# Attention plus gated MLP on one core: split value-weight loads, V and K products by column half, and fixed PSUM banks for the attention products

## The chip, the cores and the metric

The kernel runs on one core of a Trainium2 chip. The metric is the device time of one execution in microseconds (us), as the median of several runs. Single profiled executions give a trace; their span is 1.5 to 2 us shorter than the time, because the time also covers starting and ending the program.

PE is TensorE, ACT ScalarE, DVE VectorE, POOL GpSimd, SP the engine that issues all loads and stores on its one queue.

## The reference

A layer norm of x (2048 tokens, 640 features) feeds two branches, a linear attention with softmax feature maps (32 heads of 20) and a gated MLP (inner width 1536). Both are added to x. Cut to what matters:

```python
xn  = layernorm(x)
qkv = xn @ wqkv                      # q, k, v: 32 heads of 20
phi = lambda u: concat(softmax(u @ w_phi), softmax(-(u @ w_phi)))
kv  = phi(k)^T v ;  z = sum of phi(k) over the tokens       # per head
o   = phi(q) kv / (phi(q) z + 1e-6)
out = x + o @ wo + (silu(xn @ w1) * (xn @ w3)) @ w2
```

## The kernel before

The kernel does not multiply q and k by `w_phi`. It folds `w_phi` into the weights: the **first fold** makes `Wkp` for K, the **second fold** makes `Wqp` for Q. Each fold needs its part of wqkv transposed (`wqkT`), which a transposing load brings. Tiles of 128 tokens are numbered 0 to 15. K8 is the K product of tile 8, V8 its V product, ten matmuls of 320 columns each. An **MLP chunk** is one call of `mlp`: ten matmuls of 512 columns.

The parts that the change and the argument touch (cuts marked with `# ...`):

```python
class _Program:
    # ... records every operation with what it reads and writes, finds the dependencies
    def ready(self, ops):            # when PE could start these ops without waiting inside them
        t, off = 0.0, 0.0
        for o in ops:
            if o.eng != "PE":
                continue
            for d in self.find_deps(o):
                t = max(t, d.end + 0.07 - off)
            off += o.cost
        return t
    def commit(self, ops):
        # ...
            if o.dma:
                # ... one model of the queue: a rate, and a fixed time to land
                self.bus = max(self.bus, t + 0.5) + o.cost / (280e3 if o.part else 320e3)
                o.end = self.bus + 1.6

def first_loads():
    load_x(0, 1)
    load_x(1, 2)
    load_x(2, 4)
    P.dma("SP", wv[:], wqkv_t[:, :, 2 * D:3 * D])
    w13(0, 512)                                  # first third of w1 and w3: chunks 0 to 3
    P.dma("SP", phi_s[:], phi_t)
    P.dma("SP", wqkT[:, DC:2 * DC, :], A_wqkv[:, D:2 * D], True)     # for the first fold
    load_x(4, 8)
    load_x(8, 12)

def proj(t, w, k):                               # V and K products of one token tile
    for i in range(DC):                          # DC = 5 row chunks of the weights
        for q in range(2):                       # 2 column halves, one PSUM bank each
            mm(bank(k + q, 320), xnT[:, i, t * 128:(t + 1) * 128],
               w[:, i, 320 * q:320 * q + 320], i == 0, i == DC - 1)

def banks(n):                                    # the n neighbouring banks that come free first
    # ...

def loads():
    # ... for t in 4 to 15: transpose x tile t into xnT by DMA; and among them:
        if t == 7:
            yield lambda: (w13(512, 1024), load_x(12, 16))
        if t == 9:
            yield lambda: w13(1024, 1536)
            yield lambda: P.dma("SP", wqkT[:, 0:DC, :], A_wqkv[:, 0:D], True)   # second fold

def attention():
    # ... V0 to V3; then, after the first fold:
    for t in range(T):
        # ...
        yield lambda t=t: k_tile(t, banks(2))
        if t >= 4:
            yield v(t)
        if 9 <= t < 14:
            while done["f"] < 2:
                yield None
            yield lambda dc=t - 9: fold_mm(0, dc, banks(2))          # second fold, in five parts
    # ... Q products, kv sums, then the attention products of each token tile:
            yield lambda t=t: q_tok(t, banks(4))

# the scheduler: of all streams, take the operation that can start first in the model
streams = [norms(), fold_k(), attention(), k_norms(), loads(), o_transposes(), mlps(), outs()]
# ... at = max(P.ready(ops), P.free["PE"] + 0.15); the smallest (at, rank) is committed
```

So the order of instructions on each engine is not written down anywhere. A greedy scheduler makes it when the program is built, from its own estimates. The built order can be read without a chip.

The softmax here doesn't subtract the row's maximum and nothing guards it: scores larger than these inputs give would overflow.

## Time and profile before

| | before |
|---|---|
| time, median of 3 runs | 282.44 us (282.38 to 283.45) |
| span of the profiled run | 280.7 us |
| PE busy | 98% of the span |
| PE's waits, sum | 3.6 us, all before 15.6 us |
| granted TensorE clock | 1.0 |

Lines of the page of the kernel before: first the busy time of the engines (us, share of the span, instructions), then the granted clock in 40 slices (9 is 90% or more), then the chain of work that ended last, as shares by engine and line.

```profile
PE 274.5 (98%) x1890; PEld 168.4 (60%) x1890; DVE 182.7 (65%) x320; ACT 106.9 (38%) x191; POOL 59.1 (21%) x90
...
PEclk9999999999999999999999999999999999999999
...
PE PS L101 94%; DMA wqkT<-in_A_wqkv_dram 4%; SPq L113 2%; DVE xres L101 0%
```

PE is the limit, and once it has started properly nothing holds it up. The view of PE's waits (who waited for whom: us in total, times, longest) says where it was held up at all:

```profile
PE PS L101 <- DVE t_68 L101: 1.3, 1, 1.3
PE PS L101 <- DMA wv<-in_A_wqkv_dram: 0.9, 1, 0.9
PE PS L101 <- DVE x_tok L101: 0.8, 2, 0.6
PE PS L101 <- DMA wqkT<-in_A_wqkv_dram: 0.6, 1, 0.6
```

The timeline of PE (start in us, duration, operation with its tiles, count; in brackets the idle time before it and what ended it). Matmuls overlap in the trace and their ends are modelled, so the next line starts a little before a line ends (1.36 us after the start of a line of 1.52 us). The distance of two starts is the real cost: ten 320-column matmuls take 1.36 us, an MLP chunk 2.16 us.

```profile
8.77 1.52 PE L101 MATMUL PS<-wv,xnT 128*128 128x320 bf16 x10 [0.93 <-DMA wv<-in_A_wqkv_dram]
...
15.54 1.89 PE L101 MATMUL PS<-BDc,wqkT 128*128 128x140 bf16 x30 [0.62 <-DMA wqkT<-in_A_wqkv_dram]
17.26 5.61 PE L101 MATMUL PS<-Wkp,xnT 128*128 128x320 bf16 x40
22.70 4.48 PE L101 MATMUL PS<-xnT,w_s 128*128 128x512 bf16 x20
27.02 1.52 PE L101 MATMUL PS<-Wkp,xnT 128*128 128x320 bf16 x10
...
37.89 2.32 PE L101 MATMUL PS<-xnT,w_s 128*128 128x512 bf16 x10
40.05 1.52 PE L101 MATMUL PS<-Wkp,xnT 128*128 128x320 bf16 x10
...
45.48 2.32 PE L101 MATMUL PS<-xnT,w_s 128*128 128x512 bf16 x10
47.82 0.48 PE L101 MATMUL PS<-BDc,wqkT 128*128 128x140 bf16 x6
```

Read it as a list: four V tiles, the first fold (`wqkT`, `BDc`), K0 to K3, two MLP chunks (`w_s` is w1 and w3), then K4/V4 and so on, one chunk at 37.89, K8 at 40.05, one chunk at 45.48, the second fold at 47.82. Four chunks stand ahead of the second fold, three ahead of K8. After 15.54 no line has a bracket.

The load queue in the same stretch, from the timeline of SP (start and time of issue; a transposing load lands later than its issue ends):

```profile
5.47 7.87 SPq L113 DMA_TRANSPOSE wqkT<-in_A_wqkv_dram  x1
...
30.84 4.03 SPq L113 DMA_TRANSPOSE xnT<-x_tok  x2
34.92 3.54 SPq L113 DMA_DIRECT2D w_s<-in_B_w_dram  x2
38.51 6.45 SPq L113 DMA_TRANSPOSE wqkT<-in_A_wqkv_dram  x1
```

The two views are read together. The load for tile 8 (the first of the two at 30.84) took 8.5 us to land, as the view of the load queue says for the stretch around it (KB each, median us to landing); a tile's transposing load with nothing ahead of it takes 2.6 us in the same trace. So it lands at 30.84 + 8.5 = 39.34, 0.7 us before K8 needs it.

```profile
xnT<-x_tok SPq DMA_TRANSPOSE x1, 8.5
```

The second `wqkT` load is issued at 38.51 and takes 9.2 us.

### The profile page before, as it was taken

The page shows a single profiled execution, that of the slowest core. Times are in us where ns is not written, and L with a number is a line of the kernel's source. Part 1 is how long each engine was busy: PE and PEld are TensorE (multiplying, and loading weights), DVE is VectorE, ACT ScalarE, POOL GpSimd, SP SyncE. Part 2 cuts the span into 40 slices and gives each one's busy share as a digit, 9 for nine tenths or more (in the row PEclk, how much of TensorE's full clock was granted, in tenths as well). Part 3 has the DMA queues.
Part 4 walks back from the last instruction along what each step waited for, and adds up shares of the span by engine and source line. Part 5 has one row for each costly group of instructions (what it writes and reads, how often), then busy time and mean ns, then how long its engine had stood idle before and what let it go on. Part 6 is the DMA issues. An engine that isn't in the chain of part 4 may idle for free.

```text
span 280.7 us, 4627 instructions
## 1 busy us (share of the span) xinstructions
PE 274.5 (98%) x1890; PEld 168.4 (60%) x1890; DVE 182.7 (65%) x320; ACT 106.9 (38%) x191; POOL 59.1 (21%) x90
## 2 busy tenths in 40 slices
PE   7899999999999999999999999999999999999996
PEld 2665765775469655555555565744446777777774
DVE  5469969999564689989989997886663212121212
ACT  3379969888520354464464522132221000000000
POOL 4417466999951000000000000000000000000000
PEclk9999999999999999999999999999999999999999
DMA  6973899630000672211111321230000131222211
GB/s 205 282 219 62 235 267 218 92 116 2 0 0 2 206 147 44 29 25 23 26 33 37 26 47 48 60 83 1 2 0 0 50 92 56 86 66 76 71 49 47
DMA packets 39654, 21.96 MB, mean 78 GB/s; under 512 B 26704, under 2 KB 39632, under 8 KB 39632
## 3 DMA queue, kind: packets, MB, share of 16 engines
q1 hardware_dynamic: 39632, 21.66, 32.0%
q8 instruction: 15, 0.25, 0.4%
q14 instruction: 7, 0.06, 0.1%
HBM read 12.81 MB, written 2.62 MB: 55 GB/s over the span
## 4 chain that ended last, share of the span: by engine, by line
PE 94%; DMA 4%; SPq 2%; issue 0%; DVE 0%
PE PS L101 94%; DMA wqkT<-in_A_wqkv_dram 4%; SPq L113 2%; DVE xres L101 0%
## 5 line engine op out<-in xcount | busy, mean ns | idle before, releaser
L101 PE MATMUL PS<-xnT,w_s 128*128 128x512 bf16 x480 | 106.7, 379 | 0.0
L101 PEld LDWEIGHTS PS<-xnT,w_s 128*128 128x128 bf16 x480 | 46.8, 98 | 55.5
L101 ACT ACTIVATE th<-PS 128x512 f32<-128x512 f32 x48 | 28.7, 597 | 57.9 <-PE PS L101 57.9
L101 DVE TENSOR_TENSOR xres<-PS,xres 128x640 bf16<-128x640 f32 (+2 forms) x17 | 13.4, 785 | 54.0 <-PE PS L101 54.0
L101 DVE SCALAR_TENSOR_TENSOR t_68<-th,PS 128x512 bf16<-128x512 f32 x48 | 32.8, 683 | 17.2 <-ACT th L101 17.2
L101 POOL TENSOR_TENSOR ekt<-ekt,rS_62 128x640 bf16<-128x640 bf16 x32 | 39.5, 1271 | 2.3 <-DVE rS_62 L101 2.3
L101 PE MATMUL PS<-wv,xnT 128*128 128x320 bf16 x160 | 24.2, 299 | 0.9 <-DMA wv<-in_A_wqkv_dram 0.9
L101 PE MATMUL PS<-wo_s,oT 128*128 128x320 bf16 (+2 forms) x160 | 24.5, 299 | 0.0
L101 DVE TENSOR_TENSOR prod<-PS,g_s 128x1280 bf16<-128x1280 f32 x16 | 23.9, 1491 | 0.6
L101 PE MATMUL PS<-Wkp,xnT 128*128 128x320 bf16 x160 | 23.9, 299 | 0.1
L101 PE MATMUL PS<-xnT,Wqp 128*128 128x512 bf16 x100 | 23.7, 379 | 0.0
L101 DVE TENSOR_REDUCE S_61<-ekt 128x64 f32<-128x1280 bf16 x16 | 23.0, 1438 | 0.0
L101 ACT ACTIVATE ekt<-PS 128x640 bf16<-128x640 f32 x32 | 20.7, 699 | 5.3 <-PE PS L101 5.0
L101 PEld LDWEIGHTS PS<-wv,xnT 128*128 128x128 bf16 x160 | 15.5, 98 | 6.9 <-ACT xnT L101 1.1
L101 PEld LDWEIGHTS PS<-wo_s,oT 128*128 128x128 bf16 x160 | 15.6, 98 | 6.1
L101 PEld LDWEIGHTS PS<-Wkp,xnT 128*128 128x128 bf16 x160 | 15.3, 98 | 6.3 <-ACT ekt L101 0.2
L101 DVE BATCH_NORM_STATS2 bst<-x_tok 128x6 f32<-128x320 bf16 x32 | 15.2, 476 | 5.4 <-DMA x_tok<-in_A_x_dram 4.9
L101 ACT ACTIVATE e_s<-PS 128x64 f32<-128x64 f32 x32 | 9.0, 282 | 21.9 <-PE PS L101 20.9
L101 PEld LDWEIGHTS PS<-xnT,Wqp 128*128 128x128 bf16 x100 | 9.4, 98 | 8.8
L101 PE MATMUL PS<-w_s,hT_79 128*128 128x320 bf16 (+2 forms) x96 | 13.9, 299 | 0.0
L101 PE MATMUL PS<-w_s,hT_71 128*128 128x320 bf16 x96 | 13.7, 299 | 0.0
L101 PE MATMUL PS<-w_s,hT_76 128*128 128x320 bf16 x96 | 13.7, 299 | 0.0
(59 smaller groups left out, 265.7 us busy)
## 6 DMA issues: line engine op xcount, KB each, us to landing
w_s<-in_B_w_dram SPq DMA_DIRECT2D x6, 640.0 KB, 7.4
xres<-in_A_x_dram SPq DMA_DIRECT2D x16, 160.0 KB, 2.4
out_dram<-xres SPq DMA_DIRECT2D x15, 160.0 KB, 1.8
x_tok<-in_A_x_dram SPq DMA_DIRECT2D x3, 640.0 KB, 5.8
w_s<-in_B_w_dram SPq DMA_DIRECT2D x1, 1920.0 KB, 9.4
wv<-in_A_wqkv_dram SPq DMA_DIRECT2D x1, 800.0 KB, 6.4
wo_s<-in_A_wo_dram SPq DMA_DIRECT2D x1, 800.0 KB, 4.7
x_tok<-in_A_x_dram SPq DMA_DIRECT2D x2, 160.0 KB, 2.3
```

The costliest lines, as they stand in the source:

```text
L101: o = _Op(eng, lambda: m(*args, **kw), r, w, cost)
L113: o = _Op(eng, lambda: m(out, in_), self.regions(in_), self.regions(out), nbytes, True)
```

## The change

The intent: V can begin when half of its weights are there, so load wv in two column halves ahead of token tile 3, and compute V and K one column half after the other. Use the same four PSUM banks for every tile's attention products. The scheduler's estimate of the load rate was lowered as well. `LAG` only moved.

```diff
-                self.bus = max(self.bus, t + 0.5) + o.cost / (280e3 if o.part else 320e3)
+                self.bus = max(self.bus, t + 0.5) + o.cost / (280e3 if o.part else 305e3)
 ...
-        load_x(2, 4)
-        P.dma("SP", wv[:], wqkv_t[:, :, 2 * D:3 * D])
+        load_x(2, 3)
+        for a in (0, 320):
+            P.dma("SP", wv[:, :, a:a + 320], wqkv_t[:, :, 2 * D + a:2 * D + a + 320])
+        load_x(3, 4)
 ...
-        for i in range(DC):
-            for q in range(2):
+        for q in range(2):
+            for i in range(DC):
                 mm(bank(k + q, 320), xnT[:, i, t * 128:(t + 1) * 128],
 ...
-                yield lambda t=t: q_tok(t, banks(4))
+                yield lambda t=t: q_tok(t, 0)
```

The built order of PE around the loads, before and after (M is an MLP chunk, F1 and F2 the folds; in the middle, KV is a K and a V product):

```
before: V0-V3  F1    K0-K3  M M  KV4 KV5 KV6 KV7  M  K8V8 K9V9  M  F2 ...  5 M  kv sums
after:  V0-V3  F1 M  K0-K3  M    KV4 KV5 KV6 KV7     K8V8 K9V9  M  F2 ...  6 M  kv sums
```

## The prediction

> **What bounds it.** TensorE. The page gives PE 98% of the 280.7 us span; the chain of waits is PE alone from 15.54 us to 278.25. PE's waits are 3.6 us in all, all before 15.54; the last (0.6 us) is for the transposed load of wqkT (lands 15.40), which starts the K fold. Then matmuls stand back to back: twenty 512-column ones take 4.32 us (216 ns each), ten 320-column ones 1.36 us. The Trainium skill ("TensorE: Matmul & The Clock Gate", Back-to-back issue gap) gives N/2.4 + 2.5 ns, the same numbers: regrouping cannot speed them up.
>
> **What the change does.**
> 1. wv in halves, ahead of x tile 3; V by column half. V of tile 0 waits 0.9 us for wv (timeline, 8.77 us). It can start about 1 us earlier, and the four V tiles end up to 1 us earlier. But the K fold still follows them and waits for wqkT: the gain becomes a longer wait there. Worth 0.
> 2. Two more loads are issued before wqkT (about 0.47 us of queue time each) and wv moves in 640-byte runs. The skill ("DMA: Bandwidth & Descriptors", How a descriptor splits into AXI transactions) says that unaligned runs cost extra beats; the second half starts 128 bytes off a 256-byte boundary. No run shows this yet. The stretches from 4 to 11 us move 280 to 370 GB/s: the queue is busy. I estimate wqkT lands 0.0 to 0.8 us later (mean 0.3).
> 3. V and K by column half: same matmuls, same pitch; evictions still wait for both halves. 0.
> 4. Attention products always in banks 0 to 3: products are 5 to 6 us apart, their reading takes about 3 us, PE's order is unchanged. 0, at most 0.3.
> 5. The scheduler's changed DMA rate and loads reshuffle 15 to 60 us. Before: K fold, K0-3, two MLP chunks, K4/V4 to K7/V7, one MLP chunk, K8. After: K fold, one chunk, K0-3, one chunk, K4/V4 to K9/V9, then a chunk. So K8 is wanted one chunk (2.16 us) earlier: 37.89 instead of 40.05 us. In the trace the transposed load of xnT tile 8 is issued at 30.84 and takes 8.5 us, behind w1, w3 and x, so it lands at 39.34. Its predecessors on the queue depend on the layer norm of tiles 6 and 7, which I work out to finish as early as before. So K8 should wait about 1.0 to 1.5 us for that load. PE is full to the end, so nothing gives it back.
>
> **Sum.** 282.44 + 0.3 (fold later) + 1.2 (wait at K8) = 283.9 us, 8 in 10 between 282.5 and 285.0. Chances: faster by over 2% 0.01, within 2% 0.97, slower by over 2% 0.02.
>
> **What shows it.** Timeline: first V about 1 us earlier, the wait before the fold grown to over 1 us, fold start 15.5 to 16.4. PE's waits: a new one of 1.0 to 1.5 us for the xnT load, at about 38 us, just before K8. Group table: MATMUL means unchanged (379, 299 ns). No PE wait in the attention stage.
>
> **What would make it wrong.** Tile 8's load landing early (layer norms of tiles 6 and 7 done sooner): then within 0.5 us of before, or a little less if the first loads go smoother. Bank conflicts on banks 0 to 3, with VectorE 90% busy between 120 and 180 us: then 1 to 3 us more.

## The result, and the profile after

| | before | after |
|---|---|---|
| time, median of 6 runs each | 282.41 us (281.78 to 283.45) | 284.08 us (283.74 to 284.86) |
| ratio | 1 | 1.0063, 95% interval 1.0039 to 1.0086 |
| span of the profiled run | 280.7 us | 282.5 us |
| chain of waits, PE's share | 94% | 84% |

A ratio here and below is the mean time of one kernel's runs over the mean of the other's runs of the same rounds, so it is not quite the ratio of the medians. The change made the kernel about 0.6% slower.

From the page after, the chain of work that ended last, by engine and line (the counterpart of the last line shown of before; PE is again busy for 98% of the span, at a granted clock of 1.0):

```profile
PE PS L101 84%; DMA wqkT<-in_A_wqkv_dram 7%; SPq L113 3%; ACT ekt L101 3%; ACT x_tok L101 2%; ACT v_82 L101 0%; ACT th L101 0%; DVE xres L101 0%
```

PE's waits after:

```profile
PE PS L101 <- DMA wqkT<-in_A_wqkv_dram: 1.7, 2, 1.1
PE PS L101 <- DVE t_68 L101: 1.3, 1, 1.3
PE PS L101 <- ACT v_82 L101: 0.8, 1, 0.8
PE PS L101 <- DVE x_tok L101: 0.5, 2, 0.4
```

Two are new: one for ACT v_82 (0.8 us), and a second one for a `wqkT` load (1.7 us in two waits, of which 1.1 is at the first fold). The PE timeline has them in place:

```profile
7.92 1.52 PE L101 MATMUL PS<-wv,xnT 128*128 128x320 bf16 x10
9.81 0.45 PE L101 MATMUL PS<-ident,x_tok 128*128 128x128 bf16 x5 [0.36 <-DVE x_tok L101]
...
15.71 1.88 PE L101 MATMUL PS<-BDc,wqkT 128*128 128x140 bf16 x30 [1.09 <-DMA wqkT<-in_A_wqkv_dram]
17.43 2.32 PE L101 MATMUL PS<-xnT,w_s 128*128 128x512 bf16 x10
19.59 5.60 PE L101 MATMUL PS<-Wkp,xnT 128*128 128x320 bf16 x40
25.02 2.32 PE L101 MATMUL PS<-xnT,w_s 128*128 128x512 bf16 x10
...
36.69 1.52 PE L101 MATMUL PS<-wv,xnT 128*128 128x320 bf16 x10
39.02 1.52 PE L101 MATMUL PS<-Wkp,xnT 128*128 128x320 bf16 x10 [0.81 <-ACT v_82 L101]
...
44.45 2.32 PE L101 MATMUL PS<-xnT,w_s 128*128 128x512 bf16 x10
47.38 0.48 PE L101 MATMUL PS<-BDc,wqkT 128*128 128x140 bf16 x6 [0.61 <-DMA wqkT<-in_A_wqkv_dram]
```

V0 starts at 7.92 instead of 8.77. But tile 2's transposes at 9.81 wait, and the first fold starts at 15.71, as late as before, after a longer wait (1.09 us). K8 at 39.02 waits 0.81 us. The page puts this down to ACT's eviction of V7, which happened to end just then. In the program, K8's first matmul waits for its load of xnT and for an older eviction, not for this one; two other runs with the same PE order around K8 (column halves only, and column halves with fixed banks, below) name the xnT load for the same wait. The second fold, which did not wait before, waits 0.61 us.

The load queue after:

```profile
6.23 7.31 SPq L113 DMA_TRANSPOSE wqkT<-in_A_wqkv_dram  x1
...
30.42 5.02 SPq L113 DMA_TRANSPOSE xnT<-x_tok  x2
35.48 2.50 SPq L113 DMA_DIRECT2D w_s<-in_B_w_dram  x2
38.03 6.45 SPq L113 DMA_TRANSPOSE wqkT<-in_A_wqkv_dram  x1
```

The load for tile 8 is issued at 30.42, takes 8.5 us again and lands at 38.92, 0.1 us before K8 starts. The second `wqkT` load is issued at 38.03, takes 9.2 us and lands at 47.24; the fold starts at 47.38.

The chain of waits in order of time (start, us, what) shows which of the waits the end depends on. It runs through ACT's evictions and normalisations and the load queue into the second `wqkT` load, and from there through PE to the end:

```profile
38.03 9.22 DMA wqkT<-in_A_wqkv_dram
...
47.97 232.04 PE PS L101 x1590
```

K8's wait is not on this chain. The sum can be read off the second fold. Before, it starts at 47.82 with four chunks done. After, it starts at 47.38 with three chunks done. So PE has 2.16 us less work behind it and is only 47.82 − 47.38 = 0.44 us earlier: a loss of 1.72 us. From there to the end both are full; in the chain of waits the last addition starts at 278.27 us before and at 280.03 us after, 1.76 us apart.

The other profiled runs below agree with this split. From the start of the second fold to the end of the span it is 232.7 to 233.1 us in the five runs with four chunks ahead of the fold, 235.1 us in the three with three (without the run of column halves alone, which has a loss of its own later), and 230.7 to 230.8 us in the three with five. So the time behind the fold is set by the number of chunks alone. When the fold can start is less steady: with three or four chunks ahead of it the second `wqkT` load was issued anywhere between 37.06 and 39.09 us, so the 0.44 us belongs to this pair of profiles.

### The profile page after: what moved, and what is told of

Same layout as the page of the kernel before. It is cut to its first block, busy times and chain, and to the rows that moved or that the text cites. A ratio compares the mean times of both kernels' runs of the same rounds, so it can differ in the third digit from the quotient of the medians. Undisturbed runs are those within 1.5% of the kernel's fastest.

```text
span 282.5 us, 4630 instructions
## 1 busy us (share of the span) xinstructions
PE 275.5 (98%) x1890; PEld 169.0 (60%) x1890; DVE 183.7 (65%) x322; ACT 105.0 (37%) x189; POOL 59.3 (21%) x90
## 4 chain that ended last, share of the span: by engine, by line
PE 84%; DMA 7%; ACT 5%; SPq 3%; issue 0%; DVE 0%
PE PS L101 84%; DMA wqkT<-in_A_wqkv_dram 7%; SPq L113 3%; ACT ekt L101 3%; ACT x_tok L101 2%; ACT v_82 L101 0%; ACT th L101 0%; DVE xres L101 0%
```

## Experiments

All kernels gave correct results. The first four shared the runs of one kernel before (median 281.94 us), the next four those of another (282.42 us), the last four a third (281.86 us). "Chunk placement" means two or three tests added to the streams, which hold an operation back until a number of chunks is placed. They only hold back: no dependency is removed.

### Column halves alone

The kernel before with only the exchange of the two loops in `proj`. In the built orders this exchange alone reproduces the new order of the changed kernel around the folds; each of the other three parts alone, and any mixture of them without it, leaves it as before. (Built, not run: with the exchange in K alone the order changes too, with V alone it doesn't.) The scheduler's `ready` explains it. By row chunk, K0's first two matmuls need one chunk of `Wkp`, and the fifth chunk is needed at the ninth matmul. By column half all five chunks are needed within the first five matmuls, so in the model K0 is ready later, and an MLP chunk goes first.

```diff
-        for i in range(DC):
-            for q in range(2):
+        for q in range(2):
+            for i in range(DC):
```

> The kernel before with one part of the change alone: V and K products by column half. In the built order this part by itself moves an MLP chunk ahead of K0 and takes one of the four chunks away from in front of the second fold (three are left, as in the changed kernel). Theory A (the loss is one chunk of 2.16 us missing in front of the second wqkT load, and column halves alone cause it): time like the changed kernel's, 283.8 to 284.4 us, PE waits just before K8 and before the second fold that sum to 1.2 to 1.8 us. Rival B (the prediction's: the scheduler's DMA rate and the split loads cause the reshuffle, column halves are worth 0): like before, 282.2 to 282.7.

Measured: 290.95 us, ratio 1.0317 (1.0298 to 1.0337). The waits near the folds are there: 0.97 us at K8, named as the xnT load, and 0.55 us at the second fold. But 9 us is far over what either theory expected. The PE timeline of this run shows the rest near 170 us:

```profile
170.76 1.60 PE L101 MATMUL PS<-KVc,EqT 128*128 128x154 bf16 x24
174.65 0.86 PE L101 MATMUL PS<-KVc,EqT 128*128 128x154 bf16 x12 [2.28 <-DVE prod L101]
177.71 2.85 PE L101 MATMUL PS<-wo_s,oT 128*128 128x320 bf16 x10 [2.20 <-DVE prod L101]
180.35 4.34 PE L101 MATMUL PS<-w_s,hT 128*128 128x320 bf16 x24
```

At 170.76 two attention products follow one another (24 matmuls), then comes a third, and the third and the output tile after it wait 2.28 and 2.20 us for DVE's `prod`, the last reader of their banks. The stretches of 2 us (the columns after the bounds are the length and the busy us of PE, PEld, DVE, ACT and POOL with counts, then the granted clock, then DMA share and GB/s) show what follows:

```profile
176.00:178.00 2.00, 0.29 (x2) 0.18 (x3) 1.93 (x3) 0.00 (x0) 0.00 (x0) 0.50 0.55 101
...
180.00:182.00 2.00, 2.00 (x10) 1.10 (x8) 1.21 (x2) 0.00 (x0) 0.00 (x0) 0.50 0.00 0
182.00:184.00 2.00, 2.00 (x16) 1.39 (x15) 0.00 (x0) 0.00 (x0) 0.00 (x0) 0.95 0.00 0
```

The granted clock falls to 0.50 and stays there for over 6 us (the stretches before and after these read 0.85, from 174 us, and 0.95, from 182 us), and the 34 matmuls from 177.71 to 184.75 take 7.04 us. The changed kernel does the same pair of groups in 182.11 − 177.49 = 4.62 us. So the tail costs 4.48 us of waits and 2.4 us of slow clock, together 6.9 us of the 9. The Trainium skill ("TensorE: Matmul & The Clock Gate", Why this matters for your kernels) warns of this: "No PE-idle gaps >~3µs between matmul bursts". Here two gaps of 2.3 and 2.2 us with 0.86 us of work between them were enough.

### Everything but column halves

```diff
-        for q in range(2):
-            for i in range(DC):
+        for i in range(DC):
+            for q in range(2):
```

(on the changed kernel)

> The changed kernel with V and K products back in the old order; split loads, DMA rate and fixed banks stay. The built PE order is that of before. Theory A: 282.3 to 282.8 us, no PE wait after 16 us; the first fold starts 0.1 to 0.3 us later than before. Rival B: like the changed kernel, 284.1. Rival C (fixed banks cost time): over 283.

Measured: 282.81 us, ratio 1.0035 (1.0017 to 1.0053). The times expected were set from a kernel before at 282.4 us; in these rounds it ran at 281.94, so the ratio has to decide. Its middle lies between before and the whole change, and its interval overlaps that of the change. So the time alone fits theory A no better than rivals B and C; the next runs have to settle B and C. In the trace the wait at K8 is gone, as theory A says. The second fold, however, waits, which A did not expect: the second `wqkT` load was issued at 38.89 here, against 38.51 before.

```profile
48.24 0.47 PE L101 MATMUL PS<-BDc,wqkT 128*128 128x140 bf16 x6 [0.61 <-DMA wqkT<-in_A_wqkv_dram]
```

From there to the end of the span it is 281.2 − 48.24 = 232.96 us; before it is 280.7 − 47.82 = 232.88 us. So nothing behind the fold costs time, and what this kernel loses it loses ahead of the fold. Why the load was issued later, this run doesn't tell. The lower load rate exchanges four DVE operations in the built order; the orders of PE, ACT and POOL are those of before.

### The missing chunk put back

The changed kernel, with K8 held until three chunks are placed and the second fold until four are.

```diff
+            while nmlp[0] < {8: 3}.get(t, 0):
+                yield None
             yield lambda t=t: k_tile(t, banks(2))
 ...
-                while done["f"] < 2:
+                while done["f"] < 2 or nmlp[0] < {9: 4}.get(t, 0):
                     yield None
```

> The changed kernel whole, but the scheduler is made to place three MLP chunks before K8 and four before the second fold, as before. Theory A: both waits vanish; second fold starts at about 47.8 us; time 282.2 to 282.7. If the loss is in the column halves, the banks or the loads themselves: still about 284.

Measured: 282.05 us, ratio 1.0009 (0.9993 to 1.0025). The second fold starts at 47.48 without a wait, and neither is there one at K8.

```profile
47.48 0.48 PE L101 MATMUL PS<-BDc,wqkT 128*128 128x140 bf16 x6
```

Column halves, split loads, fixed banks and the lower rate are all still in this kernel; only the place of the chunk differs from the changed kernel. So the loss is where the chunk stands, and in this order the four parts together cost at most 0.25% (the end of the interval). It is not quite the order of before: one chunk still stands ahead of K0. The second `wqkT` load was issued at 37.54 here, and between 38.30 and 39.09 in the four profiled runs in which K0 follows the fold at once (before, the last experiment, fixed banks alone, split loads alone). That earlier load is how this kernel can be faster than the one of the last experiment; why it is earlier was not tested.

### The chunk moved only to the front of K8

As above, but the third chunk stands before K8 and none between V9 and the second fold: three chunks ahead of each.

```diff
+            while nmlp[0] < {8: 3}.get(t, 0):
+                yield None
 ... and in mlps(), so that no fourth chunk comes before the second fold, a chunk waits while:
+               nmlp[0] >= {8: 3, 9: 3, 10: 3}.get(done["k"], 99)
```

> The changed kernel, with the chunk that stands after V9 moved to before K8: three chunks before K8 as in before, still three before the second fold. Theory A1 (the two waits do not add: the second wqkT load sets the time of the second fold): the wait before K8 vanishes, the one before the second fold grows from 0.6 to about 1.6 us, time as the changed kernel, 283.9 to 284.3. A2 (the prediction: the wait at K8 is what costs): time falls by 0.8 to 1.0 us, to 283.1 to 283.3.

Measured: 284.20 us, ratio 1.0088 (1.0063 to 1.0113), no better than the changed kernel. K8 does not wait any more. The second fold waits more (PE timeline of this run):

```profile
47.09 0.47 PE L101 MATMUL PS<-BDc,wqkT 128*128 128x140 bf16 x6 [1.39 <-DMA wqkT<-in_A_wqkv_dram]
```

0.61 us have become 1.39 us. The two waits do not add: the load for the second fold sets the time by which PE must have work, and a wait at K8 on the way there only uses up a part of the same slack. A1 holds; A2, the prediction's own account, falls.

### Fixed banks alone

```diff
-                yield lambda t=t: q_tok(t, banks(4))
+                yield lambda t=t: q_tok(t, 0)
```

> The kernel before with the fixed banks 0 to 3 for the attention products alone. Theory: the matmul order is almost that of before, no new PE wait, ratio to before 0.998 to 1.002. If fixed banks cost something by themselves: PE waits for VectorE in the stretch from 95 to 185 us and a ratio over 1.004.

Measured: 281.91 us, ratio 0.9989 (0.9971 to 1.0007). No effect by itself, and no wait for DVE. The second fold waits 0.33 us for its load in the profiled run (283.16 us, the slowest of the six): with only 0.1 us to spare, the order of before does not always escape this wait either.

### Split loads alone

```diff
-        load_x(2, 4)
-        P.dma("SP", wv[:], wqkv_t[:, :, 2 * D:3 * D])
+        load_x(2, 3)
+        for a in (0, 320):
+            P.dma("SP", wv[:, :, a:a + 320], wqkv_t[:, :, 2 * D + a:2 * D + a + 320])
+        load_x(3, 4)
```

> The kernel before with the split wv loads and the moved x tile alone; PE, VectorE and ScalarE orders are those of before. Theory: the first wqkT load lands 0.2 to 0.8 us later than in the runs of before, and the wait at the first fold (and perhaps a small one at the second) carries it to the end: ratio 1.001 to 1.003. If the split loads are free or helpful: ratio 1.000 or less.

Measured: 282.49 us, ratio 1.0004 (0.9988 to 1.0019). The expected cost is not seen; neither is a gain. The first fold starts at 15.46 in this run. That start varies by itself: with the old loads it was 15.54, 14.61, 15.81 and 14.70 us in four profiled runs. So a shift of 0.3 us cannot be read from a pair of profiles. V0's start varies as well: 7.81 us here, but with the old loads 8.77, 7.84, 9.05 and 7.89 us in the same four runs. So the V0 that starts 0.85 us earlier in the changed kernel's profile is not shown to come from the split: with the old loads, too, wv was there by 7.9 us in two of the four.

### Column halves and fixed banks

Both loops and banks changed, old loads and old rate.

```diff
-        for i in range(DC):
-            for q in range(2):
+        for q in range(2):
+            for i in range(DC):
 ...
-                yield lambda t=t: q_tok(t, banks(4))
+                yield lambda t=t: q_tok(t, 0)
```

> Column halves and fixed banks on the kernel before; old loads, old DMA rate. Theory: the 9 us of column halves alone came from three attention products in a row without MLP chunks between them near 170 us, which the scheduler does not build with fixed banks; so the PE waits for VectorE vanish, and what stays is the waits at K8 and at the second fold, 1.2 to 1.8 us: ratio 1.004 to 1.007, the same as the changed kernel or slightly less. If column halves cost time in themselves (bank writes, weight loads): a ratio over 1.015.

Measured: 283.72 us, ratio 1.0050 (1.0030 to 1.0071). The bad tail is gone. What is left is the changed kernel's loss: 1.46 us at K8 (named as the xnT load) and 0.53 us at the second fold. So fixed banks do matter in the change: they keep the scheduler from building the tail that column halves would otherwise bring.

### One chunk ahead of the first fold

The changed kernel with the first fold held until one chunk is placed, K8 until four, the second fold until five. The chunk needs only w1 and w3, which come before `wqkT` on the queue.

```diff
     def fold_k():
+        while nmlp[0] < 1:
+            yield None
 ... K8 waits for {8: 4}, the second fold for {9: 5}, as in the missing-chunk kernel
```

> The changed kernel with one MLP chunk ahead of the first fold, four before K8 and five before the second fold. The chunk needs only the first w1 and w3 loads, which land before wqkT. Theory: PE no longer waits at the first fold (0.5 to 1.1 us in the runs so far), nor at K8, nor at the second fold; ratio to before 0.995 to 0.998, about 1 us less than before. If starting later with the fold delays the layer norms and so the loads, it is given back: ratio 1.000 or more.

Measured: 281.41 us, ratio 0.9963 (0.9948 to 0.9979). PE's waits in this run:

```profile
PE PS L101 <- DVE t L101: 1.3, 1, 1.3
PE PS L101 <- DVE x_tok L101: 1.0, 2, 0.8
```

All waits for `wqkT` and xnT loads are gone. What is left is the very start, and 0.81 us at tile 2's transposes.

### The second wqkT load issued earlier

```diff
-                yield lambda: w13(1024, 1536)
                 yield lambda: P.dma("SP", wqkT[:, 0:DC, :], A_wqkv[:, 0:D], True)
+                yield lambda: w13(1024, 1536)
```

(on the changed kernel, with the two counters that go with the loads moved too)

> The changed kernel with the second wqkT load issued ahead of the last w1 and w3 loads (the scheduler then puts the third chunk behind the second fold's first part). Theory (the load queue sets the time of the second fold): wqkT lands 2 to 4 us earlier, the wait at the second fold shrinks to under 0.3 us, the one at K8 stays near 0.9 us; 0.5 to 0.8 us less than the changed kernel, ratio to before 1.002 to 1.005. If the second fold waits for something else, no change: ratio 1.006 to 1.009.

Measured: 284.25 us, ratio 1.0058 (1.0015 to 1.0100); the runs of before scattered more in this set. PE timeline of this run:

```profile
38.65 1.52 PE L101 MATMUL PS<-Wkp,xnT 128*128 128x320 bf16 x10 [0.62 <-DMA xnT<-x_tok]
...
44.08 0.48 PE L101 MATMUL PS<-BDc,wqkT 128*128 128x140 bf16 x6
...
47.22 1.52 PE L101 MATMUL PS<-Wkp,xnT 128*128 128x320 bf16 x10 [0.50 <-DMA xnT<-x_tok]
```

The load is issued at 35.16, takes 7.3 us and lands at 42.46, 4.8 us earlier than in the changed kernel. The second fold at 44.08 does not wait. But the next K tile now waits 0.50 us at 47.22, for its xnT load, which stands behind w1 and w3 on the queue. The wait has mostly moved to the next thing on the same queue. That the queue sets the fold's time is shown; the expected gain is not, and with this interval neither is its absence.

### The kernel before with one chunk ahead of the first fold

The chunk placement of the last but one, on the kernel before; no part of the change.

```diff
     def fold_k():
+        while nmlp[0] < 1:
+            yield None
 ... K8 waits for {8: 4}, the second fold for {9: 5}
```

> The kernel before with the chunk placement of the run chunk-first (one MLP chunk ahead of the first fold, four before K8, five before the second fold), and no part of the change. Its built order has, near 170 us, three attention products in a row behind one another, like the run of column halves alone. Theory (that tail is what cost 7 us there, not the column halves): the start gains 0.5 to 1 us and the tail loses 6 to 7 us with PE waits for VectorE's prod of 4 to 5 us: ratio 1.018 to 1.024. If column halves themselves cost the time: ratio 0.996 to 0.999.

Measured: 288.16 us, ratio 1.0203 (1.0161 to 1.0245). The same tail as with column halves alone, with the same waits for `prod` (2.28 and 2.19 us), though no product is by column half. So the 7 us belong to that order of attention products, whatever made the scheduler build it.

### One chunk first, x tiles 2 and 3 together

```diff
-        load_x(2, 3)
+        load_x(2, 4)
         for a in (0, 320):
             P.dma("SP", wv[:, :, a:a + 320], wqkv_t[:, :, 2 * D + a:2 * D + a + 320])
-        load_x(3, 4)
```

(on the kernel with one chunk ahead of the first fold)

> The run chunk-first with x tiles 2 and 3 loaded together ahead of the wv halves, as before. Theory: in the changed kernel tile 2's transposes wait 0.4 to 0.8 us, because VectorE's statistics of the late tile 3 stand ahead of tile 2's normalisation; with x first that wait goes, the first V still starts by 8.2 us, and up to 0.4 us is gained: ratio 0.994 to 0.997. If wv's first half then comes too late, the V wait takes it back: ratio as chunk-first, 0.996 to 0.998.

Measured: 280.70 us (280.50 to 280.88), ratio 0.9936 (0.9895 to 0.9976), the lowest median (its interval overlaps that of the next kernel, and that of the kernel it was made from, which ran in other rounds). PE's waits:

```profile
PE PS L101 <- DVE t L101: 1.3, 1, 1.3
PE PS L101 <- DVE x_tok L101: 0.5, 2, 0.4
```

The 0.81 us at tile 2's transposes are gone. So the part "wv ahead of token tile 3" had given back there most of what an earlier V0 won. In DVE's order tile 3's statistics stand ahead of tile 2's normalisation. In the kernel this one was made from they waited 1.04 us for the later load, and tile 2's normalisation began at 9.60 us; here they do not wait, and it begins at 8.40 us.

### The same placement on the kernel before, with fixed banks

```diff
+        while nmlp[0] < 1:
+            yield None
 ... K8 waits for {8: 4}, the second fold for {9: 5}
-                yield lambda t=t: q_tok(t, banks(4))
+                yield lambda t=t: q_tok(t, 0)
```

> The run before-with-chunk-first plus fixed banks for the attention products, nothing else of the change. The built order has no three attention products in a row. Theory (fixed banks protect the tail of the order): no PE wait for VectorE's prod, ratio 0.996 to 0.999; compared with chunk-first on the changed kernel it shows what column halves and split loads add: within 0.2%.

Measured: 280.94 us (280.68 to 281.82), ratio 0.9950 (0.9904 to 0.9995). Without column halves and without split loads it is within 0.2% of the fastest kernel. The gain is the placement of the chunks, together with fixed banks to guard the tail.

## Why the prediction was right or wrong

The time was right: 283.9 us predicted, 284.08 us measured, inside the range. That it came so close is in part luck: of the two terms that made it, 0.3 us was not shown and 1.2 us rested on a wrong account.

- **What bounds the kernel.** Right. PE is full from the first fold on in the kernel before, and matmuls cost the same before and after (379 and 299 ns in the group table of both). The Trainium skill ("TensorE: Matmul & The Clock Gate", Back-to-back issue gap) gives N/2.4 + 2.5 ns, 216 ns for 512 columns, as the gap of an isolated matmul. For a sustained stream the same section has about 131 ns; this trace's stream has 216. So only waits and placement could change the time.
- **"the K fold still follows them and waits for wqkT: the gain becomes a longer wait there. Worth 0."** Right for the worth: V0 began 0.85 us earlier, the wait at the first fold grew from 0.6 to 1.1 us, and split loads alone had a ratio of 1.0004. That the split brought the earlier V0 is not shown, since V0 scatters from 7.84 to 9.05 us with the old loads.
- **"wqkT lands 0.0 to 0.8 us later (mean 0.3)".** Not shown. It is 0.17 us in the pair of profiles, but the start of the first fold scatters by over a microsecond between runs, and split loads alone cost nothing measurable.
- **"V and K by column half: same matmuls, same pitch ... 0."** Right for the matmuls, wrong as the place of the cause. **"The scheduler's changed DMA rate and loads reshuffle 15 to 60 us"** is the attribution that failed. The reshuffle was seen correctly in the built order and put down to the wrong part of the change. Column halves alone make it, and rate, loads and banks without them don't. Four builds would have told this without a chip.
- **"So K8 should wait about 1.0 to 1.5 us for that load. PE is full to the end, so nothing gives it back."** The wait is there, 0.81 us, a little under the range; its load took the 8.5 us that were expected and landed at 38.92. But as the account of the loss this step failed. It missed that the second fold has its own load, with 0.1 us of slack before, and that the chunk had left the stretch ahead of it too. Moving the chunk in front of K8 removed K8's wait and left the time as it was; the wait came back as 1.39 us at the second fold. The right sum is one chunk (2.16 us) less what the second `wqkT` load came earlier (0.44 us), 1.72 us. The predicted 0.3 + 1.2 came out close by its sum, not by its parts, which is luck. What holds of it is the kind of cause: PE ran out of work ahead of a late load.
- **Fixed banks, "0, at most 0.3".** Right for the changed kernel and for fixed banks alone. Not foreseen: without them column halves would have cost 9 us.

What stays open: why the kernel without column halves is about 1.0 us slower than before (its second `wqkT` load comes later, and its second fold waits 0.61 us; the cause of the later load was not found, and the lower rate was not run alone), and whether issuing the second `wqkT` load earlier helps a little.

## What to carry to other kernels

When one engine is full, look for the loads that land just before they are needed: the distance between landing and use is the slack that any reordering spends. Waits behind one queue need not add: here the one that ended last counted. Where a scheduler makes the order, build each part of a change alone and compare the orders before explaining anything; an edit that is neutral in itself can move work at the other end of the program. Give the full engine independent work (here one MLP chunk) ahead of each late load, and check that it is still there after every edit.

## What the Trainium skill lacked or had wrong

- "TensorE: Matmul & The Clock Gate" (Why this matters for your kernels) puts the limit at idle gaps of about 3 us. Here no single gap was that long: 2.28 and 2.20 us with 0.86 us of matmuls between them brought the granted clock to 0.50 for over 6 us. (The page's section A second HAM failure mode: psum-queue depth-cycling tells of short idles that do this when they are frequent, without a length.) The half and full clock of its section What's actually happening agree: the stretches show 0.50 and 1.00, and 0.85 and 0.95 only as means over a change.
- "DMA: Bandwidth & Descriptors" (How a descriptor splits into AXI transactions) counts extra beats for runs that do not start 256-byte aligned, and gives no time for them; the prediction estimated a cost from it. Loading wv in 640-byte halves, of which the second starts 128 bytes off, had no measurable effect on the kernel's time: ratio 1.0004 (0.9988 to 1.0019).
- The same page's section DMA Transpose (X-bar) gives no time for one that stands behind plain loads on the same queue. Here a 160 KB one took 2.6 us by itself and 8.5 us behind three loads of 640 KB each.
- None of the pages used says how much the first loads scatter from run to run. Here the same load order started its first fold between 14.61 and 15.81 us.
